# Projections with a contraction of 64: from a zero-padded 128-row matmul to two 64-row tiles

## The chip, the core and the metric

The kernel runs on one core of one Trainium2 chip. The time is device microseconds of that core, from several runs; beside it there is one profiled execution, from which all views of the trace come.

## What is computed

A linear attention with a feature map, and a gated feed-forward layer on its output. Shapes: q, k, v are 8 batches x 8 heads x 576 positions x 64; `w_phi` is 64 x 128; the feed-forward layer takes 4608 x 512 through 512 x 1536 (twice) and 1536 x 512.

```python
def phi(x):
    proj = np.einsum('bhsd,df->bhsf', x, w_phi)              # contraction over 64
    proj = proj - np.max(np.abs(proj), axis=-1, keepdims=True)
    return np.concatenate([np.exp(proj), np.exp(-proj)], axis=-1)
q_p, k_p = phi(q), phi(k)
kv = np.einsum('bhsf,bhsd->bhfd', k_p, v);  z = np.sum(k_p, axis=2)
num = np.einsum('bhsf,bhfd->bhsd', q_p, kv)
den = np.einsum('bhsf,bhf->bhs', q_p, z)[..., None] + 1e-06
x = (num / den)                                              # to (4608, 512)
out = (np.maximum(x @ w_gate, 0) * (x @ w_val)) @ w_out
```

## The kernel before

**Tiles.** Of the 576 positions of a head 512 make four chunks of 128; the last 64 of two batches make one "mixed" block. Input blocks hold two chunks (or two heads, in the mixed blocks) of 64 columns side by side, 128 x 128. `transposed` (L126) turns four or eight such blocks on TensorE (L131) and copies them to SBUF (L135). A turned block then holds the first chunk's 64 features on partitions 0 to 63 and the second's on 64 to 127; the first is called even here, the second odd.

**Projection by rows.** `project_rows` (L138) multiplies a turned block (stationary, 128 x 128) by `w2` (L505), which is two 128-column halves: `w_phi` on the upper 64 rows with zeros below, and zeros above with `w_phi` on the lower 64. A matmul of 256 columns (L142) so gives both chunks of a block side by side; two of them fill one PSUM bank, and one `tensor_reduce` (L147) takes the four largest absolute values. A K item (`k_start`, `k_rows`, `k_values`, `k_kv`) calls it twice, and each call is followed on ScalarE by two exponentials of 512 columns (L177, `kp`); after the second come two small ones of the maxima (L184, `ek`). A K item covers two heads of one batch; there are 32, and four mixed ones. `k_values` scales V by `ek` on GpSimd (L159), and `k_kv` (L204) sums 20 matmuls (L218).

**Projection by columns.** A Q item needs the rows only for its maxima (`q_rows`, L229; `cq`, L233), and the projection itself by columns: `q_cols` (L235) has one half of `w2` as the stationary operand and four turned blocks, 512 columns, as the moving one (L241), then two exponentials (L247, `qp`). A Q item covers two chunks of a batch and all heads: four row calls and four column calls. There are 16, and four mixed ones with half of that. `q_num` (L253) then does 16 matmuls of 65 columns a chunk (L263), VectorE adds the two halves (L279, L287) and takes a reciprocal (L290), GpSimd scales (L292, `xu`), and `q_finish` (L296) turns the result (L299, L305) into `xT`.

**Feed-forward.** `ffn_slices` (L309) cuts a batch's layer into slices: 12 pairs of a val and a gate slice, four matmuls of 512 columns each (L320), and twelve slices of four matmuls for the output (L342; a bank is taken by the first of three). A val slice is copied by ScalarE (L329), a gate slice is worked off by VectorE (L331). For batch 0 half of the pairs are cut into slices of 256 columns.

**What sets the order.** Nothing reorders: `at(tick, fn, ...)` puts each step on a fixed grid, and all steps are issued in the order of ticks (L576), at the same tick in the order of entry. From tick 36 on each tick has one feed-forward slice. A K item starts every four ticks: transposes at t0, row calls at t0+2 and t0+3, V at t0+5, `k_kv` at t0+10 (L389). A Q item has row calls at t0+2 to t0+5 and column calls at t0+4 to t0+7 (L420); the first two have ticks by hand (L518 to L527). PSUM has five banks under the tag `pa` for the attention (`ps_a`) and three under `pf` (`ps_f`), taken in turn.

Of the kernel before, what the change touches and what calls it, by code (L numbers as in the profile page):

```python
# [8 lines left out]
FP32 = mybir.dt.float32  # L9
BF16 = mybir.dt.bfloat16  # L10
# [6 lines left out]
def kernel(  # L17
# [24 lines left out]
    P = 128  # L42
# [92 lines left out]
        nc.vector.tensor_copy(t.rearrange("p a b -> p (a b)"), pt[:, 0 : n * P])  # L135
        return t

    def project_rows(T2, m):  # L138

        pp = psum_a()  # L140
        for i in range(2):
            nc.tensor.matmul(  # L142
                pp[:, 2 * F * i : 2 * F * (i + 1)],
                lhsT=T2[:, i, :],
                rhs=w2.rearrange("p a f -> p (a f)"),
            )
        nc.vector.tensor_reduce(  # L147
            m,
            pp.rearrange("p (c f) -> p c f", f=F),
            axis=AX.X,  # L150
            op=ALU.max,
            apply_absolute_value=True,
        )
        return pp

    def scale_v(engs, dst, src, ek):

        for s, eng in enumerate(engs):
            eng.tensor_tensor(  # L159
                dst[:, :, s, 0:D],  # L160
                src,
                ek[:, :, s : s + 1].to_broadcast([P, 8, D]),
                op=ALU.mult,
            )
        engs[0].tensor_copy(dst[:, :, :, D], ek)
# [4 lines left out]
        st["kp"] = []  # L170
        st["m"] = sb_s.tile([P, 8], FP32, name="mk")

    def k_rows(st, i):
        pp = project_rows(st["T"][:, 2 * i : 2 * i + 2], st["m"][:, 4 * i : 4 * i + 4])
        kp = st["pool"].tile([P, 2, 4, F], BF16, name=f"kp{i}")
        for s, sign in ((0, 1.0), (1, -1.0)):
            nc.scalar.activation(  # L177
                kp[:, s].rearrange("p c f -> p (c f)"), pp, AF.Exp, scale=sign
            )
        st["kp"].append(kp)  # L180
        if i == 1:
            ek = st["ek"] = sb_s.tile([P, 8, 2], FP32, name="ek")
            for s, sign in ((0, -1.0), (1, 1.0)):
                nc.scalar.activation(ek[:, :, s], st["m"], AF.Exp, scale=sign)  # L184

    def k_values(st, b, u, engs):
        vs = st["vs"] = sb_k.tile([P, 8, 2, E], BF16, name="vs")
        vn = inputs["vn", b][:, 2 * u : 2 * u + 2].rearrange("p h c d -> p (h c) d")
        scale_v(engs, vs, vn, st["ek"])

    def k_values_mixed(st, i, bb, engs):

        ekm = sb_s.tile([P, 8, 2], FP32, name="ekm")
        nc.vector.tensor_scalar(
            ekm.rearrange("p a b -> p (a b)"),
            st["ek"].rearrange("p a b -> p (a b)"),
            half[:, bb : bb + 1],
            None,
            op0=ALU.mult,
        )  # L200
        vs = st["vs", bb] = sb_mix.tile([P, 8, 2, E], BF16, name=f"vsm{bb}")
        scale_v(engs, vs, inputs["vm", i], ekm)

    def k_kv(st, b, u, copy):  # L204
        mixed = km_state[b // 2]
        pk = psum_a()
        kv_ps = pk[:, 0 : 4 * E].rearrange("p (h s e) -> p h s e", h=2, s=2)
        n = 0
        for hh in range(2):
            h = 2 * u + hh  # L210
            for s in range(2):
                for c in range(C + 1):
                    if c < C:
                        lhsT, rhs = st["kp"][hh][:, s, c, :], st["vs"][:, 4 * hh + c, s, :]
                    else:
                        lhsT = mixed["kp"][h // 4][:, s, h % 4, :]
                        rhs = mixed["vs", b % 2][:, h, s, :]
                    nc.tensor.matmul(  # L218
                        kv_ps[:, hh, s, :], lhsT=lhsT, rhs=rhs, start=(n == 0), stop=(n == 19)
                    )  # L220
                    n += 1
        kv = kvs[b, u] = sb_kv.tile([P, 2, 2, E], BF16, name="kv")
        copy(kv.rearrange("p h s e -> p (h s e)"), pk[:, 0 : 4 * E])  # L223

    def q_start(st, blocks):
        st["T"] = transposed(blocks)
        st["m"] = sb_s.tile([P, 2 * len(blocks)], FP32, name=f"mq{len(blocks)}")

    def q_rows(st, i):  # L229
        project_rows(st["T"][:, 2 * i : 2 * i + 2], st["m"][:, 4 * i : 4 * i + 4])  # L230
        if 4 * i + 4 == st["m"].shape[1]:
            st["c"] = sb_s.tile(st["m"].shape, FP32, name="cq")
            nc.scalar.activation(st["c"], st["m"], AF.Exp, scale=2.0)  # L233

    def q_cols(st, x, slot, lo, par, first):  # L235

        if "qp" not in x:
            x["qp"] = sb_f.tile([P, 2, 2, 4, P], BF16, name="qp", bufs=4)
            x["u"] = sb_f.tile([P, 8, E], FP32, name="u")
        pf = psum_f() if first else psum_a()  # L240
        nc.tensor.matmul(  # L241
            pf,
            lhsT=w2[:, par, :],
            rhs=st["T"][:, lo : lo + 4].rearrange("p a b -> p (a b)"),
        )
        for s, sign in ((0, 1.0), (1, -1.0)):
            nc.scalar.activation(  # L247
                x["qp"][:, s, slot].rearrange("p a b -> p (a b)"), pf, AF.Exp, scale=sign
            )

    GROUPS = ((0, 3), (3, 3), (6, 2))

# [136 lines left out]
    def k_item(t0, b, u, t_kv=0, engs=POOL, copy=nc.scalar.copy):  # L389
        st = {}  # L390

        def start():
            kn = inputs["kn", b]
            blocks = [
                kn[:, 2 * u + i // 2, 2 * (i % 2) : 2 * (i % 2) + 2, :].rearrange("p c d -> p (c d)")
                for i in range(4)
            ]
            k_start(st, blocks, sb_k)

        at(t0, start)  # L400
        at(t0 + 2, k_rows, st, 0)
        at(t0 + 3, k_rows, st, 1)
        at(t0 + 5, k_values, st, b, u, engs)
        at(max(t0 + 10, t_kv), k_kv, st, b, u, copy)

    def k_item_mixed(t0, i, engs=POOL):
        st = km_state[i] = {}

        def start():
            km = inputs["km", i]  # L410
            blocks = [km[:, 2 * j : 2 * j + 2, :].rearrange("p h d -> p (h d)") for j in range(4)]
            k_start(st, blocks, sb_mix)

        at(t0, start)
        at(t0 + 2, k_rows, st, 0)
        at(t0 + 3, k_rows, st, 1)
        at(t0 + 6, k_values_mixed, st, i, 0, engs)
        at(t0 + 22 if i else 44, k_values_mixed, st, i, 1, POOL)

    def q_item(t0, blocks, cols, chunks, ticks=None, **how):  # L420


        n = len(chunks)
        if ticks is None:
            ticks = dict(
                rows=[t0 + 2 + i for i in range(2 * n)],
                cols=[t0 + 4 + i for i in range(2 * n)],
                num=[t0 + 6 + 2 * n + 3 * ci for ci in range(n)],
                end=[t0 + 12 + 2 * n + 3 * ci for ci in range(n)],
            )  # L430
        st, xs = {}, [{} for _ in chunks]
        at(t0, lambda: q_start(st, blocks()))
        for i in range(2 * n):
            at(ticks["rows"][i], q_rows, st, i)
            ci, slot, lo, par = cols[i]
            at(ticks["cols"][i], q_cols, st, xs[ci], slot, lo, par, bool(how))
        for ci, (batches, place, col, dst) in enumerate(chunks):
            for j in range(3):
                at(
                    ticks["num"][ci] + j,  # L440
                    *(q_num, st, xs[ci], j, batches, place, col, how.get("t_act", False)),
                )
            at(ticks["end"][ci], lambda x=xs[ci], dst=dst: q_finish(x, dst()))
            last["q"] = ticks["end"][ci]

    def q_item_chunks(t0, b, cp, **how):
# [6 lines left out]
        def dst(c):  # L453
            if b not in xTs:
# [3 lines left out]
        q_item(  # L458
            t0,
            blocks,  # L460
            [(ci, half_, 4 * half_, ci) for ci in range(2) for half_ in range(2)],
            [
                (
                    (b,),
                    lambda h: (h // 4, h % 4),
                    lambda h, ci=ci: 2 * h + ci,
                    lambda ci=ci: dst(2 * cp + ci),
                )
                for ci in range(2)
# [4 lines left out]
    def q_item_mixed(t0, i):  # L474
        def blocks():
# [3 lines left out]
        q_item(  # L479
            t0,  # L480
            blocks,
            [(0, par, 0, par) for par in range(2)],
            [
                (
                    (2 * i, 2 * i + 1),
# [16 lines left out]
    load_v(0, 2, H, nc.gpsimd)  # L502
    load_mixed(0, "km", k, nc.gpsimd, BF16)
    load_q(0)
    w2 = singles.tile([P, 2, F], BF16)  # L505
    nc.vector.memset(w2, 0.0)
    half = singles.tile([P, 2], FP32)
    nc.vector.memset(half, 0.0)
    for hh in range(2):
        rows = slice(D * hh, D * (hh + 1))  # L510
        nc.vector.memset(half[rows, hh : hh + 1], 1.0)
        nc.vector.tensor_copy(w2[rows, hh, :], wf[rows])


    for u in range(NU):
# [1 line left out]
    k_item_mixed(16, 0, DVE)  # L517
    q_item_chunks(  # L518
        *(17, 0, 0),
        ticks=dict(cols=[20,20,20,21], rows=[20, 20, 22.5, 22.5], num=[27,30], end=[33.5,35]),  # L520
        t_act=True,
    )
    q_item_chunks(
        *(19, 0, 1),
        ticks=dict(cols=[33,33,34,34], rows=[26,29,32,35], num=[39,42], end=[45,47.5]),
        t_act=False,
    )  # L527
    S0 = 36
# [79 lines left out]
```

## Time and profile before

| | |
|---|---|
| median of 3 runs | 430.24 us (429.47 to 430.27) |
| span of the profiled execution, first to last instruction | 426.3 us |
| between that span and the median of the runs | 3.9 us |
| TensorE busy | 398.7 us, 94%, 3357 records of matmuls |
| VectorE busy | 284.1 us, 67% |
| ScalarE busy | 250.9 us, 59% |
| GpSimd busy | 159.6 us, 37% |
| granted TensorE clock, mean | 0.998 |

The profile page gives, in order, the busy time of each engine, the same in forty slices of the span (10.7 us each, tenths of busy), the DMA queues, and the chain of work that ended last. A line of a timeline has the start in us from the span's start, the length, the engine, the line of the kernel, the operation, the tiles (written <- read) and the number of instructions merged into it. Matmuls overlap in their records: the length of one is more than its distance to the next. A few records of matmuls are missing (a group of four may show three).

### The profile page before, as it was taken

How to read it: one execution, taken by the hardware profiler on the slowest of the kernel's cores; microseconds unless marked ns; L12 is line 12 of the kernel's file. 1: busy time of each engine (PE TensorE's matmuls, PEld its weight loads, DVE VectorE, ACT ScalarE, POOL GpSimd, SP SyncE). 2: the span in 40 equal slices, each digit the busy share in tenths (PEclk: the TensorE clock that was granted, in tenths of full speed). 3: DMA queues.
4: the chain of work that ended last, by engine and by line, in shares of the span. 5: the costliest groups of instructions: out<-in, count | busy, mean ns of one | idle time of the engine just before them, and what ended most of it. 6: DMA issues, size and time to landing. Idle time of an engine off the chain costs nothing.

```text
span 426.3 us, 8695 instructions
## 1 busy us (share of the span) xinstructions
PE 398.7 (94%) x3357; PEld 232.9 (55%) x3416; DVE 284.1 (67%) x641; ACT 250.9 (59%) x575; POOL 159.6 (37%) x204
## 2 busy tenths in 40 slices
PE   3777899989999999999999999999999999999995
PEld 1556665645556556555566556555565554444442
DVE  4888569867687679866876699676856795330420
ACT  3984776566667755687567665766667552322321
POOL 8953861176217501574155211870362021000000
PEclk9999999999999999999999999999999999999999
DMA  8997795245413750167015901374020002002004
GB/s 157 199 265 164 108 181 61 75 122 59 56 51 98 128 61 2 61 156 94 2 59 160 116 3 52 71 139 51 26 76 2 1 14 86 2 0 100 0 2 98
DMA packets 45337, 33.66 MB, mean 79 GB/s; under 512 B 12848, under 2 KB 40112, under 8 KB 45296
## 3 DMA queue, kind: packets, MB, share of 16 engines
q0 software_dynamic: 30480, 16.52, 28.1%
q1 hardware_dynamic: 14816, 16.58, 12.4%
q8 instruction: 27, 0.44, 0.4%
q14 instruction: 14, 0.11, 0.1%
HBM read 37.81 MB, written 9.44 MB: 111 GB/s over the span
## 4 chain that ended last, share of the span: by engine, by line
PE 78%; DVE 10%; ACT 4%; POOL 2%; issue 2%; DMA 2%; POOLq 0%; DVEq 0%; ACTq 0%
PE pf L320 40%; PE pf L342 17%; PE pa L142 6%; PE pa L218 5%; PE pa L263 4%; PE pa L241 3%; PE pa L131 3%; DVE u L287 2%; DVE mk L147 2%; DMA qn_117<-in_q_dram 2%; DVE t L279 2%; PE pa L299 1%; POOL xu L292 1%; ACT qp L247 1%; ACT t L275 1%
## 5 line engine op out<-in xcount | busy, mean ns | idle before, releaser
L320 PE MATMUL pf<-xT,wv_sb 128*128 128x512 bf16 (+1 forms) x386 | 96.9, 366 | 3.8 <-DVE xT L305 2.6
L320 PE MATMUL pf<-xT,wg_sb 128*128 128x512 bf16 (+1 forms) x394 | 97.7, 366 | 2.0 <-ACT val_sb L329 1.4
L292 POOL TENSOR_TENSOR xu<-u,r 128x512 bf16<-128x512 f32 x36 | 37.5, 1042 | 164.1 <-DVE r L290 128.9
L329 ACT CAST val_sb<-pf 128x512 bf16<-128x512 f32 (+1 forms) x114 | 65.3, 573 | 52.7 <-PE pf L320 52.3
L247 ACT ACTIVATE qp<-pa 128x512 bf16<-128x512 f32 x128 | 69.5, 604 | 11.9 <-PE pa L241 11.9
L320 PEld LDWEIGHTS <-wg_sb 128*128 128x128 bf16 x456 | 44.4, 98 | 41.6 <-issue 2.1
L320 PEld LDWEIGHTS <-wv_sb 128*128 128x128 bf16 x456 | 43.3, 98 | 36.5 <-issue 3.9
L147 DVE TENSOR_REDUCE mk<-pa 128x4 f32<-128x512 f32 x72 | 48.4, 682 | 11.3 <-PE pa L142 11.1
L263 PEld LDWEIGHTS <-qp 128*128 128x128 bf16 x640 | 33.9, 98 | 21.5 <-issue 0.9
L287 DVE TENSOR_TENSOR u<-pa,t 128x195 f32<-128x195 f32 (+3 forms) x120 | 40.5, 338 | 6.8 <-ACT t L275 0.5
L279 DVE TENSOR_TENSOR t<-pa,cq 128x195 f32<-128x195 f32 (+3 forms) x114 | 37.6, 330 | 4.6 <-PE pa L263 3.8
L352 ACT COPY out_sb<-pf 128x512 f32<-128x512 f32 x36 | 21.3, 592 | 32.4 <-PE pf L342 29.5
L263 PE MATMUL pa<-kv,qp 128*128 128x65 bf16 x640 | 37.9, 193 | 0.9 <-DVE u L287 0.5
L331 DVE SCALAR_TENSOR_TENSOR h_6277<-pf,val_sb 128x512 bf16<-128x512 f32 x12 | 8.3, 692 | 22.8 <-PE pf L320 22.8
L331 DVE SCALAR_TENSOR_TENSOR h_6056<-pf,val_sb 128x512 bf16<-128x512 f32 x12 | 8.3, 692 | 14.5 <-PE pf L320 14.5
L299 PEld LDWEIGHTS <-xu 128*128 128x128 bf16 x144 | 10.7, 98 | 11.7 <-POOL xu L292 3.8
L223 ACT CAST kv<-pa 128x260 bf16<-128x260 f32 x28 | 10.7, 380 | 10.0 <-PE pa L218 9.9
L299 PE MATMUL pa<-ident,xu 128*128 128x128 bf16 x144 | 14.0, 219 | 2.1 <-POOL xu L292 1.6
L331 DVE SCALAR_TENSOR_TENSOR h_566<-pf,val_sb 128x256 bf16<-128x256 f32 (+1 forms) x18 | 9.1, 506 | 8.8 <-ACT val_sb L329 4.1
L331 DVE SCALAR_TENSOR_TENSOR h_1578<-pf,val_sb 128x512 bf16<-128x512 f32 x12 | 8.3, 691 | 9.6 <-ACT val_sb L329 5.7
L305 DVE COPY xT<-pa 128x512 bf16<-128x512 bf16 x32 | 13.3, 417 | 1.9 <-PE pa L299 1.7
L331 DVE SCALAR_TENSOR_TENSOR h_3132<-pf,val_sb 128x512 bf16<-128x512 f32 x12 | 8.2, 686 | 7.3 <-PE pf L320 3.8
(580 smaller groups left out, 776.1 us busy)
## 6 DMA issues: line engine op xcount, KB each, us to landing
out_dram<-out_sb SPq DMA_DIRECT2D x32, 256.0 KB, 2.3
wv_sb<-in_moe_w_val_dram POOLq DMA_DIRECT2D x3, 512.0 KB, 8.2
wg_sb<-in_moe_w_gate_dram POOLq DMA_DIRECT2D x3, 512.0 KB, 9.7
wo_sb<-in_moe_w_out_dram POOLq DMA_DIRECT2D x1, 1536.0 KB, 13.3
vn_1018<-in_v_dram SPq DMA_DIRECT2D x1, 1024.0 KB, 8.9
vn_335<-in_v_dram POOLq DMA_DIRECT2D x1, 1024.0 KB, 13.5
vn_1793<-in_v_dram SPq DMA_DIRECT2D x1, 1024.0 KB, 7.1
vn_2508<-in_v_dram SPq DMA_DIRECT2D x1, 1024.0 KB, 7.2
```

The source lines that it names most:

```text
L142: nc.tensor.matmul(pp[:, 2 * F * i : 2 * F * (i + 1)], lhsT=T2[:, i, :], rhs=w2.rearrange("p a f -> p (a f)"),)
L147: nc.vector.tensor_reduce(m, pp.rearrange("p (c f) -> p c f", f=F), axis=AX.X, op=ALU.max, apply_absolute_value=True,)
L247: nc.scalar.activation(x["qp"][:, s, slot].rearrange("p a b -> p (a b)"), pf, AF.Exp, scale=sign)
L263: nc.tensor.matmul(pn[:, E * (2 * i + s) : E * (2 * i + s + 1)], lhsT=x["qp"][:, s, slot, blk, :], rhs=kvs[b, h // 2][:, h % 2, s, :],)
L279: nc.vector.tensor_tensor(t, ab[:, :, 1], st["c"][rows, col(lo) : col(lo + n - 1) + 1 : col(1) - col(0)][:, :, None].to_broadcast([np_, n, ...
L287: nc.vector.tensor_tensor(x["u"][rows, lo : lo + n], ab[:, :, 0], t, op=ALU.add)
L292: nc.gpsimd.tensor_tensor(x["xu"], x["u"][:, :, 0:D], r.to_broadcast([P, 8, D]), op=ALU.mult)
L299: nc.tensor.matmul(pt[:, P * i : P * i + P], lhsT=x["xu"][:, 2 * i : 2 * i + 2].rearrange("p a d -> p (a d)"), rhs=ident, is_transpose=True,)
L320: nc.tensor.matmul(ps, lhsT=w[:, dc, P * fi : P * fi + P], rhs=xT[:, dc, lo:hi], start=(dc == 0), stop=(dc == NDC - 1),)
L329: nc.scalar.copy(st["val"], ps)
L331: nc.vector.scalar_tensor_tensor(st["h2"][:, fi, lo:hi], ps, 0.0, st["val"], op0=ALU.max, op1=ALU.mult)
L342: nc.tensor.matmul(st["po"], lhsT=st["h2"][:, fi, P * t : P * t + P], rhs=wo_sb[:, fi, :], start=(fi == 0), stop=(fi == NFC - 1),)
```

## The change

The projections no longer multiply by zeros. `wd` holds `w_phi` twice, on partitions 0 to 63 and on 64 to 127. Each matmul takes 64 partitions of the turned block and of `wd`: the even chunk from the upper half, the odd one from the lower half. In the built program these have a tile of 64 rows x 128 columns at row 0 or row 64; all other matmuls keep 128 x 128. Even and odd chunks go to two PSUM banks.

Since a bank now holds four even or four odd chunks, `project_rows` takes four blocks at once and issues eight matmuls of 128 columns and two reduces; the two row calls of a K item become one, at t0+2, and all four exponentials and both `ek` come from that one step. Row and column calls of a Q item are paired in the same way (t0+2 and t0+4; t0+4 and t0+6). The order of V's blocks, of the maxima and of the stationary blocks of `k_kv` follows. The grid of all other steps stays.

```diff
-    def project_rows(T2, m):
-        pp = psum_a()
-        for i in range(2):
-            nc.tensor.matmul(
-                pp[:, 2 * F * i : 2 * F * (i + 1)],
-                lhsT=T2[:, i, :],
-                rhs=w2.rearrange("p a f -> p (a f)"),
-            )
-        nc.vector.tensor_reduce(m, ...)
-        return pp
+    def project_rows(T4, ms):
+        pps = [psum_a(), psum_a()]
+        for i in range(4):
+            for par in range(2):
+                half_rows = slice(D * par, D * (par + 1))
+                nc.tensor.matmul(
+                    pps[par][:, F * i : F * (i + 1)],
+                    lhsT=T4[half_rows, i, :],
+                    rhs=wd[half_rows, :],
+                )
+        for pp, m in zip(pps, ms):
+            nc.vector.tensor_reduce(m, ...)
+        return pps
...
-    def k_rows(st, i):
-        pp = project_rows(st["T"][:, 2 * i : 2 * i + 2], st["m"][:, 4 * i : 4 * i + 4])
-        kp = st["pool"].tile([P, 2, 4, F], BF16, name=f"kp{i}")
-        for s, sign in ((0, 1.0), (1, -1.0)):
-            nc.scalar.activation(kp[:, s]..., pp, AF.Exp, scale=sign)
-        st["kp"].append(kp)
-        if i == 1:
-            ek = ...
+    def k_rows(st):
+        pps = project_rows(st["T"], [st["m"][:, 4 * i : 4 * i + 4] for i in range(2)])
+        for i, pp in enumerate(pps):
+            kp = st["pool"].tile([P, 2, 4, F], BF16, name=f"kp{i}")
+            for s, sign in ((0, 1.0), (1, -1.0)):
+                nc.scalar.activation(kp[:, s]..., pp, AF.Exp, scale=sign)
+            st["kp"].append(kp)
+        ek = ...
...
-        vn = inputs["vn", b][:, 2 * u : 2 * u + 2].rearrange("p h c d -> p (h c) d")
+        vn = inputs["vn", b][:, 2 * u : 2 * u + 2].rearrange("p h (c a) d -> p a (h c) d", a=2)
...
-    def q_cols(st, x, slot, lo, par, first):
+    def q_cols(st, places, lo, first):
+        pfs = []
+        for x, slot in places:
...
+            pfs.append(psum_f() if first else psum_a())
+        for par, pf in enumerate(pfs):
+            half_rows = slice(D * par, D * (par + 1))
+            nc.tensor.matmul(
+                pf,
+                lhsT=wd[half_rows, :],
+                rhs=st["T"][half_rows, lo : lo + 4].rearrange("p a b -> p (a b)"),
+            )
+        for (x, slot), pf in zip(places, pfs):
+            for s, sign in ((0, 1.0), (1, -1.0)):
+                nc.scalar.activation(x["qp"][:, s, slot]..., pf, AF.Exp, scale=sign)
...
         at(t0, start)
-        at(t0 + 2, k_rows, st, 0)
-        at(t0 + 3, k_rows, st, 1)
+        at(t0 + 2, k_rows, st)
...
-                rows=[t0 + 2 + i for i in range(2 * n)],
-                cols=[t0 + 4 + i for i in range(2 * n)],
+                rows=[t0 + 2 + 2 * i for i in range(n)],
+                cols=[t0 + 4 + 2 * i for i in range(n)],
...
-    w2 = singles.tile([P, 2, F], BF16)
-    nc.vector.memset(w2, 0.0)
+    wd = singles.tile([P, F], BF16)
...
-        nc.vector.tensor_copy(w2[rows, hh, :], wf[rows])
+        nc.vector.tensor_copy(wd[rows, :], wf[rows])
...
-        ticks=dict(cols=[20,20,20,21], rows=[20, 20, 22.5, 22.5], num=[27,30], end=[33.5,35]),
+        ticks=dict(cols=[20, 20], rows=[20, 22.5], num=[27, 30], end=[33.5, 35]),
...
-        ticks=dict(cols=[33,33,34,34], rows=[26,29,32,35], num=[39,42], end=[45,47.5]),
+        ticks=dict(cols=[33, 34], rows=[26, 32], num=[39, 42], end=[45, 47.5]),
```

In the changed program the lines are some 3 to 16 higher: L144 is the row matmul, L150 its reduce, L182 and L188 the exponentials of a K item, L255 the column matmul, L262 its exponentials, L335 the val and gate matmuls, L344 the val copy.

## The prediction on record

> **What bounds the kernel now.** I read the page first: the share of each engine, then the slices, then the chain that ended last.
>
> ```profile
> span 426.3 us, 8695 instructions
> ...
> PE 398.7 (94%) x3357; PEld 232.9 (55%) x3416; DVE 284.1 (67%) x641; ACT 250.9 (59%) x575; POOL 159.6 (37%) x204
> ...
> PE   3777899989999999999999999999999999999995
> ...
> ACT  3984776566667755687567665766667552322321
> ...
> PE 78%; DVE 10%; ACT 4%; POOL 2%; issue 2%; DMA 2%; POOLq 0%; DVEq 0%; ACTq 0%
> ```
>
> From the fifth slice (some 42 us) TensorE is full, and the chain lies on it. "Busy" can mislead, so the timeline of TensorE alone comes next: there a matmul's real price is the distance to the next start.
>
> ```profile
> 202.73 0.35 PE L263 MATMUL pa<-kv,qp 128*128 128x65 bf16 x6
> 202.92 0.38 PE L142 MATMUL pa<-w_119,tT_3454 128*128 128x256 bf16 x2
> 203.14 1.03 PE L320 MATMUL pf<-xT,wv_sb 128*128 128x512 bf16 x4
> 204.00 0.35 PE L263 MATMUL pa<-kv,qp 128*128 128x65 bf16 x6
> ...
> 205.40 0.38 PE L241 MATMUL pa<-tT_3454,w_119 128*128 128x512 bf16 x1
> 205.61 0.38 PE L142 MATMUL pa<-w_119,tT_3454 128*128 128x256 bf16 x2
> 205.83 1.03 PE L320 MATMUL pf<-xT,wv_sb 128*128 128x512 bf16 x4
> ```
>
> Start to start: two L142 take 0.22 us, one L241 0.21, a slice of four L320 0.86, and six L263, each with a weight load of its own, 0.19 (0.031 for load and matmul). Nothing is idle between them, so a microsecond of TensorE work is worth a microsecond there, as long as nothing else becomes late. What could is ScalarE and the three PSUM banks `pf`, so I looked at one K item among val and gate slices:
>
> ```profile
> 188.08 0.38 PE L142 MATMUL pa<-w_119,tT_3208 128*128 128x256 bf16 x2
> ...
> 188.30 1.03 PE L320 MATMUL pf<-xT,wv_sb 128*128 128x512 bf16 x4
> 188.50 0.69 DVE L147 TENSOR_REDUCE mk<-pa 128x4 f32<-128x512 f32 x1
> ...
> 189.23 1.08 ACT L177 ACTIVATE kp_3255<-pa 128x512 bf16<-128x512 f32 x2 [0.57 <-DVE mk L147]
> ...
> 190.20 0.59 ACT L329 CAST val_sb<-pf 128x512 bf16<-128x512 f32 x1
> ...
> 190.66 1.12 ACT L177 ACTIVATE kp_3269<-pa 128x512 bf16<-128x512 f32 x2
> ...
> 191.56 0.81 PE L320 MATMUL pf<-xT,wg_sb 128*128 128x512 bf16 x3
> 191.63 0.34 ACT L184 ACTIVATE ek<-mk 128x8 f32<-128x8 f32 x2
> 191.83 0.62 ACT L329 CAST val_sb<-pf 128x512 bf16<-128x512 f32 x1
> ```
>
> The gate slice at 191.56 takes the bank of the val slice of 188.30 (three banks: val, gate, val, then the first again). The copy that frees it ends at 190.79, because it stands between the two pairs of exponentials. The margin is 0.77 us. ScalarE's pace, start to start: a pair 0.97, both `ek` 0.20, a copy 0.46 before the next may start, 0.59 to its end.
>
> **Edit 1: the streams get shorter.** 288 row matmuls of 256 columns become 576 of 128, in 72 calls; 72 column matmuls of 512 columns become 36 pairs. A rows call costs 4 x 0.108 = 0.43 now. Side by side its four pairs would stream in 4 x 0.056 = 0.22 (eight L131 transposes, also 128 columns wide, took 0.45 from 200.55 to 201.00), but it now has eight weight loads, and the L263 pace of 0.031 gives 0.25: 0.18 saved. A column pair costs 0.43 now and 0.215 + 0.03 (the second starts a load later) then: 0.185 saved. In the full region, after 42 us, there are 63 row calls and 32 column pairs; in 13 of the row calls the saving vanishes in a wait (edit 3). Gain: 50 x 0.18 + 32 x 0.185 = 14.9 us.
>
> **Edit 2: the array changes its shape.** The built order has the 64-row work in 90 separate stretches among 128-row work, 80 of them after some 42 us and 67 outside the 13 waits; each is entered and left, 134 changes. No row of this trace has a 64-row tile. Below, a change costs nothing, as between any two matmuls above (a gain is excluded: no work goes). Above, the earlier matmul must leave altogether and the next load cannot be early: a 65-column matmul lasts 193 ns and hands over after 31, so 0.16 us remain, and a load precedes its matmul by 0.03 (L241: load 205.37, matmul 205.40): 0.19. I take 0.12, nearer to the upper row, since a change is a wait for the one before and the zero rows are all of one shape: 134 x 0.12 = +16.1 us (0 to 25.5).
>
> The rule that speaks against the change stands in the Trainium skill, "TensorEngine Tiling (Array Packing)", section Key Properties: changing the tiling mode, not just the tile, drains TensorE. It gives no price; by the rule the upper row is the truer one (25.5), by the trace's unbroken streams it would be 0.
>
> **Edit 3: four exponentials in one piece.** `k_rows` now issues both reduces, four exponentials and both `ek` before the next slice is issued. ScalarE takes its work in order, so the val copy is queued behind all six; before, behind two. Worked out on the item above with 0.12 a change: row matmuls end at 188.08 + 0.12 + 0.25 = 188.45, and the first reduce starts 0.20 later (as 188.30 to 188.50); reduces to 189.33 and 190.01, first pair at 189.37, second at 190.34, `ek` at 191.31, copy from 191.51 to 192.1. TensorE leaves the 64-row work at 188.57 and wants that bank after 0.86 + 0.86 + 0.44 + 0.86, at 191.6; it gets it 0.5 late, 0.54 after the 191.56 of before. Behind the gate matmuls stand kv and all that follows. In the built order ten K items have the pattern rows, val, gate, transposes, val, gate; four of them have half as many transposes, so that their slice came 0.22 earlier: 6 x 0.54 + 4 x 0.76 = +6.3 us (5.1 with free changes, 7.0 with 0.19). K items among output slices are free of it, since `po` takes a bank once in three slices.
>
> Three K items of batch 1 stand among the half slices (256 columns). The chain of waits has exponentials at 47.28 (kp_836) and again at 51.16 (kp_914): 3.88 an item. Afterwards: 0.20 + 0.68 + 2 x 0.97 + 0.20 + val copy 0.37 = 3.4 until the bank is free, gate 0.43, kv 0.61, rows with two changes 0.49: 4.9. That is 3 x 1.0 = +3.1 us.
>
> **Edit 4: the start.** `cq` of the second Q item now stands ahead of the eight `qp` exponentials on ScalarE (all rows come at ticks 26 and 32, before the first columns at 33); it was last, at 32.36. It waits for two reduces that VectorE reaches after the reciprocal at 29.13: 29.33 + 2 x 0.65 = 30.65, `cq` to 31.0. The eight began at 28.54 and are on the chain until 32.68, where L320 waits for them: +2.3 us. Then at 38.05 the chain goes through `kp_660` to a val copy; that now waits for one more pair and `ek`: +1.2. Together +3.5 (0 to 5).
>
> **Free, and what hides it.** Counts and sizes of reduces, exponentials, V scalings and PSUM copies stay. V is read in another order with the same 64-element runs; POOL is busy 37%, and a call of 1.05 us could be longer by a tenth before `kv`, five ticks later, sees it. The dropped memset of `w2` lies under the first load. Column exponentials now come four in a row as well; TensorE's own work between the slices (num, kv) nearly covers them: +0.5 (0, where changes are dear, to 4, where they are free). No DMA moves on its queue.
>
> **Sum.** -14.9 + 16.1 + 6.3 + 3.1 + 3.5 + 0.5 = +14.6 on the profiled span of 426.3: 440.9. The median of the runs is 3.9 above that span (430.24), which I take as unchanged: **445 us**.
>
> **Rivals.** *The gain comes through (faster).* One mechanism: the val copies are not late, since ScalarE's 59% leaves room to catch up, and a change costs little. Without waits the streams give 63 x 0.18 + 32 x 0.185 = 17.3 against 160 changes; it decides at 0.108 a change. At 0.05 the sum is -9.3, 421 us. For it: the full TensorE row. Against it: the margin of 0.77, smaller than the pair and `ek` that are put before the copy. 11%. *No side by side*: the halves stream one after the other, or their loads do not overlap; edit 1 brings nothing, 460 us. For it: nothing in this trace shows two matmuls streaming at once. 12%. *Waits, but free changes*: -14.9 + 5.1 + 2.7 + 3.5 + 4 = +0.4, some 431 us, either side of no change. For it: the unbroken streams above, though all of one shape. 17% (5 faster, 6 within 0.2%, 6 slower). *Forecast*, with changes of 0.05 to 0.19: 436 (-14.9 + 6.7 + 5.6 + 2.9 + 3.5 + 2 = +5.8) to 454 (-14.9 + 25.5 + 7.0 + 3.3 + 3.5 = +24.4), 60%.
>
> **Numbers.** Likeliest 445. The range holds the forecast and most of the two cases beside it: 430 to 460. Faster by over 0.2%, about what a measurement here can tell from none: 16%; within 0.2%: 6%; slower: 78%.
>
> **What would show it.** Edit 1: a pair of L144 starting within some 0.03 us, rows calls of about 0.25, L255 pairs under 0.25. Edit 2: a gap before the first L144 or L255 of a stretch and before the first matmul after it. Edit 3: in K items TensorE idle before the second gate slice, released by the val copy. Edit 4: `cq` waiting for a reduce near 29 to 31 us and the first full slice 2 to 4 us later. Wrong would be: no gaps at the changes, or pairs one behind the other.

## The result, and the profile after

The changed kernel takes **448.93 us** (median of 4 runs, 447.95 to 449.15), the kernel before 429.86 us beside it (4 runs): ratio 1.0448, 95% interval 1.0429 to 1.0467. It is slower, as forecast, 3.9 us above the predicted 445.0 and inside the range.

From the page of the changed kernel: span, engine shares, two of the slices, granted clock and chain. They answer to the lines shown of before.

```profile
span 446.7 us, 9336 instructions
...
PE 405.0 (91%) x3704; PEld 225.5 (50%) x3704; DVE 282.8 (63%) x640; ACT 249.0 (56%) x575; POOL 159.7 (36%) x204
...
PE   2587679988999899999999999999999999999995
...
ACT  3954566546575765566666664676566662332321
PEclk9966899999999999999999999999999999999999
...
PE 67%; DVE 18%; ACT 10%; issue 2%; DMA 1%; POOL 0%; DVEq 0%; ACTq 0%; POOLq 0%
```

The profiled span grew by 20.4 us while VectorE's and ScalarE's busy times hardly moved. TensorE's share of the chain fell from 78% to 67%, and that of VectorE and ScalarE together rose from 14% to 28%: time went into waits for them. (TensorE's busy times can't be compared: the profile of before has 3357 matmul records for 3416 weight loads, so some are missing, this one has all 3704; and some matmuls run at half clock here.) The slices show two regions, a start that is emptier, at a lower clock in the third to fifth slice, and then a full TensorE again.

To see where the 20.4 us arise I followed the same slices through both traces, by VectorE's work on each gate slice: the changed kernel is 6.0 us behind at 33 us of before, 9.6 at 46, 12.0 at 58, and 20.4 from 342 on. **12.0 lie in the start, 8.4 in the steady part.**

The medians differ by 19.1 us and not by 20.4, because the profiled execution of before was a short one: its span is 426.3 us, those of the 43 executions of before listed with the experiments are 426.6 to 429.0. The traces show where. TensorE's waits for the first loads of K, before, in the changed kernel and in e13_qonly (the last experiment below):

```profile
PE pa L131 <- DMA kn_101<-in_k_dram: 5.6, 2, 4.5
PE pa L131 <- DMA kn<-in_k_dram: 7.2, 2, 4.8
PE pa L131 <- DMA kn<-in_k_dram: 6.5, 2, 4.7
```

(us in total, times, longest.) The second of these loads is issued at 2.67 us in all three; the transposes that it releases start at 7.74, 8.93 and 8.62 us. In all 13 profiled executions of other kernels they start at 8.2 to 9.0 us, also in e5_change and e13_qonly, which leave these first steps as they were. So 1.2 of the 12.0 us are, in all likelihood, not the change's.

TensorE's timeline of the changed kernel, over a K item (row call at 204.86) and a Q item:

```profile
204.86 0.40 PE L144 MATMUL pa<-wd,tT 64*128 64x128 bf16 x8
205.19 1.04 PE L335 MATMUL pf<-xT,wv_sb 128*128 128x512 bf16 x4
206.06 1.03 PE L335 MATMUL pf<-xT,wg_sb 128*128 128x512 bf16 x4
206.92 0.61 PE L131 MATMUL pa<-ident,qn 128*128 128x128 bf16 x8
207.37 1.03 PE L335 MATMUL pf<-xT,wv_sb 128*128 128x512 bf16 x4
208.79 1.02 PE L335 MATMUL pf<-xT,wg_sb 128*128 128x512 bf16 x4 [0.40 <-ACT val_sb L344]
...
210.23 0.20 PE L224 MATMUL pa<-vsm,kp 128*128 128x65 bf16 x1
210.35 0.40 PE L144 MATMUL pa<-wd,tT 64*128 64x128 bf16 x8
210.68 1.04 PE L335 MATMUL pf<-xT,wv_sb 128*128 128x512 bf16 x4
...
212.52 0.39 PE L255 MATMUL pa<-tT,wd 64*128 64x512 bf16 x2
212.74 0.39 PE L144 MATMUL pa<-wd,tT 64*128 64x128 bf16 x8
```

Three of the prediction's signs are here. *Side by side*: two L255 and then the next call within 0.22 us, the price of one full matmul of 512 columns; start to start, the two of a pair are 3 to 4 ns apart. The section "Part 3: Packing small matmuls — row/col tiling" of the Trainium skill's page "TensorE: Matmul & The Clock Gate" gives about 4 ns between the starts of packed tiles; this trace agrees. *Gaps at a change*: from the last L224 to the first L144 it is 0.12 us, where a 65-column matmul hands over after 0.031, so the way in costs 0.095; over all stretches I read 0.095 to 0.096 in, 0.092 to 0.102 out. *The late gate slice*: from 207.37 to 208.79 a slice takes 1.42 instead of 0.86 us, 0.56 late, released by the val copy.

The waits of TensorE in the changed kernel (us in total, times, longest), the whole span:

```profile
PE pf L335 <- ACT val_sb L344: 9.8, 13, 1.7
...
PE pf L335 <- DVE xT L320: 4.4, 4, 1.5
PE pf L255 <- ACT qp L262: 4.1, 2, 2.4
PE pa L144 <- DVE u L302: 3.7, 11, 0.4
```

The first line is what the prediction was built on. The last was not in it: the row call that directly follows a column pair waits for `u`, VectorE's add of a num step. TensorE's timeline, then VectorE's in the same stretch:

```profile
222.50 0.39 PE L255 MATMUL pa<-tT,wd 64*128 64x512 bf16 x2
222.73 0.22 PE L144 MATMUL pa<-wd,tT 64*128 64x128 bf16 x1
223.35 0.39 PE L144 MATMUL pa<-wd,tT 64*128 64x128 bf16 x7 [0.40 <-DVE u L302]
```

```profile
221.35 1.28 DVE L150 TENSOR_REDUCE mq<-pa 128x4 f32<-128x512 f32 x2
222.54 0.35 DVE L294 TENSOR_TENSOR t<-pa,cq 128x195 f32<-128x195 f32 x1
222.93 0.36 DVE L302 TENSOR_TENSOR u<-pa,t 128x195 f32<-128x195 f32 x1
```

The first even matmul goes; the first odd one waits for its bank. Of the five `pa` banks the stretch takes four, after one for a num step, so its last bank is that of the num step one tick back, and its reader `u` stands on VectorE behind two reduces in one piece (1.28 us). With the matmul that waits, all seven behind it wait. Ten such waits of 0.36 to 0.57 us after 60 us make 5.0 us.

### The profile page after: what moved, and what is told of

It reads as the page before. It is cut to its first block, busy times and chain, and to the rows that moved or that the text cites. A ratio compares the mean times of both kernels' runs of the same rounds, so it can differ in the third digit from the quotient of the medians.

```text
span 446.7 us, 9336 instructions
## 1 busy us (share of the span) xinstructions
PE 405.0 (91%) x3704; PEld 225.5 (50%) x3704; DVE 282.8 (63%) x640; ACT 249.0 (56%) x575; POOL 159.7 (36%) x204
## 4 chain that ended last, share of the span: by engine, by line
PE 67%; DVE 18%; ACT 10%; issue 2%; DMA 1%; POOL 0%; DVEq 0%; ACTq 0%; POOLq 0%
PE pf L335 33%; PE pf L357 18%; ACT kp L182 7%; PE pa L224 5%; PE pa L144 4%; DVE mk L150 4%; DVE u L302 3%; DVE mq L150 3%; DVE t L294 3%; PE pa L278 2%; PE pa L131 2%; DVE h L346 2%; PE pa L255 2%; ACT val_sb L344 1%; DMA kn<-in_k_dram 1%
## 5 line engine op out<-in xcount | busy, mean ns | idle before, releaser
L346 DVE SCALAR_TENSOR_TENSOR h<-pf,val_sb 128x512 bf16<-128x512 f32 (+1 forms) x114 | 75.4, 662 | 110.2 <-ACT val_sb L344 59.9
L335 PE MATMUL pf<-xT,wg_sb 128*128 128x512 bf16 (+1 forms) x408 | 100.9, 370 | 9.8 <-ACT val_sb L344 9.8
L335 PE MATMUL pf<-xT,wv_sb 128*128 128x512 bf16 (+1 forms) x408 | 101.9, 373 | 4.4 <-DVE xT L320 4.4
L357 PE MATMUL pf<-wo_sb,h 128*128 128x512 bf16 x432 | 105.0, 379 | 0.0
L182 ACT ACTIVATE kp<-pa 128x512 bf16<-128x512 f32 x144 | 74.4, 604 | 50.1 <-DVE mk L150 49.8
L344 ACT CAST val_sb<-pf 128x512 bf16<-128x512 f32 (+1 forms) x114 | 63.9, 577 | 56.0 <-PE pf L335 56.0
L162 POOL TENSOR_TENSOR vs<-vn,ek 128x512 bf16<-128x512 f32 x64 | 65.9, 1051 | 32.8 <-ACT ek L188 32.7
L262 ACT ACTIVATE qp<-pa 128x512 bf16<-128x512 f32 x128 | 66.1, 603 | 10.3 <-PE pa L255 10.3
L335 PEld LDWEIGHTS <-wg_sb 128*128 128x128 bf16 x456 | 43.4, 99 | 55.9 <-issue 13.1
L335 PEld LDWEIGHTS <-wv_sb 128*128 128x128 bf16 x456 | 39.4, 99 | 43.2 <-issue 8.1
L357 PEld LDWEIGHTS <-h 128*128 128x128 bf16 x432 | 37.8, 98 | 36.6 <-issue 0.5
L150 DVE TENSOR_REDUCE mk<-pa 128x4 f32<-128x512 f32 x72 | 46.2, 684 | 9.6 <-PE pa L144 9.5
L150 DVE TENSOR_REDUCE mq<-pa 128x4 f32<-128x512 f32 x72 | 45.8, 678 | 0.7 <-PE pa L144 0.2
L144 PE MATMUL pa<-wd,tT 64*128 64x128 bf16 x576 | 32.9, 228 | 8.4 <-DVE tT L135 4.4
L135 DVE COPY tT<-pa 128x512 bf16<-128x512 bf16 (+1 forms) x56 | 27.3, 487 | 5.9 <-PE pa L131 5.6
L144 PEld LDWEIGHTS <-tT 64*128 64x128 bf16 x576 | 19.1, 98 | 19.6 <-DVE tT L135 6.2
```

The lines of the kernel that those rows point to most:

```text
L144: nc.tensor.matmul(pps[par][:, F * i : F * (i + 1)], lhsT=T4[half_rows, i, :], rhs=wd[half_rows, :],)
L150: nc.vector.tensor_reduce(m, pp.rearrange("p (c f) -> p c f", f=F), axis=AX.X, op=ALU.max, apply_absolute_value=True,)
L162: eng.tensor_tensor(dst[:, :, s, 0:D].rearrange("p (a b) d -> p a b d", a=2), src, ek[:, :, s : s + 1].to_broadcast([P, 8, D]).rearrange(" ...
L182: nc.scalar.activation(kp[:, s].rearrange("p c f -> p (c f)"), pp, AF.Exp, scale=sign)
L262: nc.scalar.activation(x["qp"][:, s, slot].rearrange("p a b -> p (a b)"), pf, AF.Exp, scale=sign)
L335: nc.tensor.matmul(ps, lhsT=w[:, dc, P * fi : P * fi + P], rhs=xT[:, dc, lo:hi], start=(dc == 0), stop=(dc == NDC - 1),)
```

## The experiments

Theory: the loss is made of order (val copies behind four exponentials, `cq` ahead of the `qp` exponentials, second banks not yet free), and the change of shape takes back most of what the streams gain. Rivals: tiles are dear in themselves; the start is slow because of the clock. Every ratio is to runs of the kernel before beside them, whose medians were 429.1 to 429.5 us.

| run | edit | median us | ratio, 95% interval |
|---|---|---|---|
| e3_full | changed kernel, same steps, no tiles | 451.53 | 1.0498, 1.0467 to 1.0529 |
| e5_change | kernel before, columns from 64 rows, one at a time | 443.59 | 1.0326, 1.0297 to 1.0354 |
| e1_split | changed kernel, K exponentials in two steps | 437.06 | 1.0173, 1.0147 to 1.0199 |
| e2_cq | changed kernel, `cq` after the columns | 447.14 | 1.0408, 1.0380 to 1.0436 |
| e7_split_cq | both | 434.42 | 1.0113, 1.0081 to 1.0145 |
| e4_later | changed kernel, column pairs a tick later | 457.24 | 1.0651, 1.0635 to 1.0667 |
| e6_all | e7 and e4 | 443.13 | 1.0322, 1.0301 to 1.0344 |
| e8_warm | e6 and filler matmuls in the start | 444.02 | 1.0343, 1.0321 to 1.0365 |
| e11_early | e7, joined steps ahead of num | 433.47 | 1.0088, 1.0073 to 1.0102 |
| e10_hybrid | e11, no tiles in the start | 431.06 | 1.0035, 1.0023 to 1.0047 |
| e12_kfull | e10, no tiles in K items | 431.64 | 1.0049, 1.0036 to 1.0062 |
| e13_qonly | kernel before, tiles in steady Q items only | **427.80** | **0.9967, 0.9954 to 0.9979** |

**Order without tiles (e3_full).** Pairs, banks and steps as changed, matmuls zero-padded as before.

```diff
-                    lhsT=T4[half_rows, i, :], rhs=wd[half_rows, :],
+                    lhsT=T4[:, i, :], rhs=w2[:, par, :],
...
-                lhsT=wd[half_rows, :], rhs=st["T"][half_rows, lo : lo + 4]...
+                lhsT=w2[:, par, :], rhs=st["T"][:, lo : lo + 4]...
```

> The changed kernel with its steps, pairs, banks and orders, but each projection matmul uses all 128 rows and the zero-padded weights, as before the change: no 64-row tile, no change of shape. It separates the tiles from the rearrangement. Theory (the tiles by themselves gain a little, 20 us of streaming against 15 us of changes, and the rearrangement loses): TensorE streams 20 us more and has no gaps at changes, the waits stay; 448 to 454 us. Rival (the tiles are the loss): 430 to 438 us.

TensorE's waits in it:

```profile
PE pf L333 <- ACT val_sb L342: 10.4, 13, 1.7
...
PE pf L333 <- DVE xT L318: 4.9, 4, 1.8
...
PE pf L253 <- ACT qp L260: 4.6, 2, 2.3
```

The same waits, so they belong to the order. Tiles in this order are worth 2.6 us by the medians (451.53 against 448.93) and 1.1 by the two profiled spans, where followed slice by slice 3.2 us are gained after 58 us and 2.1 lost before. They are not the cause of the slowdown, as the theory had it (448 to 454 us).

**Changes of shape alone (e5_change).** Only the 64 rows without zeros, but each by itself: no pairs, no gain, two changes for each of the 72 column matmuls.

```diff
-            lhsT=w2[:, par, :],
-            rhs=st["T"][:, lo : lo + 4]...,
+            lhsT=w2[D * par : D * (par + 1), par, :],
+            rhs=st["T"][D * par : D * (par + 1), lo : lo + 4]...,
```

> The kernel before with one edit: a column matmul takes only the 64 rows that are not padded, still one at a time, so nothing is saved and each of the 72 is entered and left. Theory (a change of shape costs 0.096 us each way, as the gaps in the changed kernel show): 64 of them lie where TensorE is full, 64 x 0.19 = 12 us more, 441 to 443 us. Rival (a change is hidden, or costs only where something else waits): 430 to 433 us.

Its TensorE timeline:

```profile
203.63 0.39 PE L241 MATMUL pa<-tT,w 64*128 64x512 bf16 x1
203.95 0.39 PE L142 MATMUL pa<-w,tT 128*128 128x256 bf16 x2
204.18 1.03 PE L320 MATMUL pf<-xT,wv_sb 128*128 128x512 bf16 x4
205.13 0.39 PE L241 MATMUL pa<-tT,w 64*128 64x512 bf16 x1
```

From L241 to the next start 0.32 instead of 0.216, and from the slice of four at 204.18 to L241 0.95 instead of 0.86. 14.1 us over 72 stretches are 0.195 each, as the gaps add up (0.096 + 0.102). The time is 0.6 us above the range that I expected, which counted the 64 stretches of the full part alone. A lone row call or column pair, which saves 0.21, about breaks even; a column pair and a row call joined in one stretch save 0.43 and pay once.

**The K exponentials (e1_split) and `cq` (e2_cq), and both (e7_split_cq).**

```diff
-        pps = project_rows(st["T"], [st["m"][:, 4 * i : 4 * i + 4] for i in range(2)])
-        for i, pp in enumerate(pps):
+        st["pp"] = project_rows(st["T"], [st["m"][:, 4 * i : 4 * i + 4] for i in range(2)])
+        k_exp(st, 0)
+    def k_exp(st, i):
+        pp = st["pp"][i]
...
+        if i == 0:
+            return
         ek = ...
...
         at(t0 + 2, k_rows, st)
+        at(t0 + 3, k_exp, st, 1)
...
-        ticks=dict(cols=[33, 34], rows=[26, 32], num=[39, 42], end=[45, 47.5]),
+        ticks=dict(cols=[33, 34], rows=[26, 35], num=[39, 42], end=[45, 47.5]),
```

> The changed kernel, but the second pair of exponentials of a K item and its two small ones are issued one tick later, so that on ScalarE the val copy again stands between the two pairs. Theory (the waits for the val copy are the larger part of the loss): TensorE's waits for the val copy, 9.8 us in the changed kernel's trace, go, and the K items of the half slices get shorter; 436 to 441 us. Rival (the changes between 64 and 128 rows are the loss, and a wait removed here returns elsewhere): 446 to 449 us.

> The changed kernel, but the second row pair of the second Q item is at tick 35, after the columns, as its last row call was before. Theory (the start is late because cq holds up the eight exponentials): cq no longer stands ahead of them, the first gate slice is worked off some 2 us earlier than the 39 us of the changed kernel, and 445 to 447 us result. Rival (the start is held by something else, the granted clock for instance): 448 to 450 us.

> As the one with three orders mended, but the column pairs stay where the change put them (t0+4 and t0+6). Theory: 437.1 - 1.8 = 434 to 436 us, above the one with all three. Rival (the pair waits cost nothing beside the two others): the same time as with all three.

The waits of TensorE in e1_split:

```profile
PE pf L261 <- ACT qp L268: 3.9, 2, 2.2
PE pa L144 <- DVE u L308: 3.7, 11, 0.4
...
PE pf L341 <- ACT val_sb L350: 1.2, 3, 0.5
```

One step moved by a tick takes 11.9 us out: the val waits fall from 9.8 to 1.2 us, the start from 12.0 to 6.9, the steady part from 8.4 to 1.5. `cq` is worth 1.8 us alone (447.14, just above the theory's 445 to 447) and 2.6 on top of e1_split. What is left in e7_split_cq is 4.6 us at 58 us and 1.5 after, so most of it is start.

**Column pairs a tick later (e4_later, e6_all): a miss.** I wanted the row call's second bank to be free.

```diff
-                cols=[t0 + 4 + 2 * i for i in range(n)],
+                cols=[t0 + 5 + 2 * i for i in range(n)],
```

> The changed kernel, but the column pairs of a Q item come one tick later (t0+5 and t0+7), so that a row pair and a column pair no longer take four PSUM banks of the attention at once. Theory (the second bank of such a row pair waits for VectorE's add of the tick before, 5.1 us in all): those waits go, and the 14 stretches that were joined fall apart, 14 x 0.19 = 2.7 us more of changes; 445 to 448 us. Rival (VectorE is the bound there, so the wait only moves): 449 to 452 us.

> The changed kernel with three orders mended together: the second pair of exponentials of a K item one tick later, the second row pair of the second Q item at tick 35, the column pairs one tick later. Theory (the losses are separate waits and add up): 437.1 - 1.8 - 2.4, some 431 to 434 us; what is left above the kernel before lies in the first 50 us. Rival (they overlap): 435 to 438 us. If the tiles' own gain (20 us of streaming against some 18 us of changes) were larger than thought, under 429 us.

It costs 8.3 us alone and 8.7 on top of e7_split_cq, more than the rivals had allowed as well. TensorE in e6_all:

```profile
216.51 0.39 PE L261 MATMUL pa<-tT,wd 64*128 64x512 bf16 x1
217.27 0.39 PE L261 MATMUL pa<-tT,wd 64*128 64x512 bf16 x1 [0.37 <-DVE u L308]
217.59 1.04 PE L341 MATMUL pf<-xT,wg_sb 128*128 128x512 bf16 x4
```

Now the column pair meets the occupied bank. Its second matmul comes 0.76 us after the first and streams alone: the wait and, on top, the whole gain of the pair. 13 such waits sum to 6.6 us, where the row calls had lost 5.0 and have 1.1 now; 14 joined stretches fall apart into two (14 x 0.19 = 2.7). That is 6.6 - 3.9 + 2.7 = 5.4 of the 8.7, and 13 lost pairings of 0.21 make another 2.7.

**The clock in the start (e8_warm): not decided.** 17 times two throwaway matmuls of 512 columns before 30 us, in e6_all.

```diff
+    for wt in (0, 2, 4, 6, 8, 10, 12, 14, 16, 17, 18, 19, 24, 26, 27, 28, 29):
+        at(wt, warm, 2)
```

> The kernel with three orders mended, plus 17 times two throwaway matmuls of 512 columns on a spare bank in the first 30 us, which only keep TensorE busy. Theory (part of the late start is the granted clock, which falls to 0.5 for some 10 to 20 us since TensorE is idle there): the clock stays at 1.0 from some 18 us on and the span gets 2 to 4 us shorter than without them; 428 to 431 us. Rival (the start waits for other engines, the clock does not matter): the same time as without, or up to 3 us more for the throwaway work.

The rows of stretches (from:to, length, busy us of TensorE, weight loads, VectorE, ScalarE and GpSimd with their instructions, granted clock, share of DMA, GB/s) in the changed kernel say what it was for:

```profile
18.40:21.80 3.40, 1.01 (x16) 0.45 (x16) 3.37 (x5) 3.39 (x9) 3.38 (x6) 1.00 1.13 169
21.80:28.60 6.80, 6.21 (x102) 5.59 (x99) 4.48 (x11) 2.92 (x7) 2.58 (x5) 0.50 1.23 259
28.60:32.00 3.40, 2.26 (x42) 1.55 (x39) 2.71 (x8) 3.08 (x16) 0.67 (x1) 1.00 1.24 220
32.00:42.30 10.30, 7.52 (x46) 4.88 (x47) 5.06 (x14) 5.09 (x13) 2.92 (x4) 0.50 0.97 208
42.30:49.10 6.80, 4.19 (x58) 3.24 (x55) 5.04 (x17) 3.17 (x9) 1.78 (x2) 1.00 0.01 2
49.10:52.50 3.40, 3.11 (x24) 2.29 (x25) 2.19 (x5) 1.74 (x4) 3.40 (x5) 0.50 0.16 36
```

TensorE gets half its clock for 20.5 us, in three stretches. Those ahead of them show it less busy: 1.01 of 3.40 us, 2.26 of 3.40, 4.19 of 6.80. The kernel before keeps 1.00 from 18 to 45 us. The Trainium skill's page "TensorE: Matmul & The Clock Gate", section "Part 1: The HAM clock gate", states half rate after an idle window of about 3.4 us; the lengths here, 3.4, 6.8 and 10.3 us, fit its multiples, but TensorE was not idle in the stretches before. The filler did not hold the clock (0.87 from 18 to 45 us against 0.75 in e6_all, then 0.89 to 60 us against 1.00) and the time stayed, 444.02 against 443.13. What the clock adds to the start remains open: no run here changes the clock there by itself.

**The joined step ahead of num (e11_early), no tiles in the start (e10_hybrid), nor in K items (e12_kfull).**

```diff
-                rows=[t0 + 2 + 2 * i for i in range(n)],
-                cols=[t0 + 4 + 2 * i for i in range(n)],
+                rows=[t0 + 2 + 1.9 * i for i in range(n)],
+                cols=[t0 + 3.9 + 2.1 * i for i in range(n)],
...
+                    lhsT=T4[:, i, :] if padded or full["now"] else T4[half_rows, i, :],
+                    rhs=w2[:, par, :] if padded or full["now"] else wd[half_rows, :],
...
+    at(36, lambda: full.update(now=False))
```

> The version with the second K pair a tick later and cq after the columns, and in Q items the joined column and row step issued ahead of the num step of its tick (rows at t0+3.9, columns at t0+3.9 and t0+6). The second bank of that row pair is then one whose reader finished two ticks before, not the num bank whose add is still to come. Theory (the bank is what the row pair waits for): the waits of L144 for the add u, 5.0 us there, go, and the time falls from 434.4 to 429.5-432. Rival (VectorE is late anyway, the wait only moves to the num step or the next column pair): 433.5-435, with waits of the same sum at other lines.

> The version before this one in the list, and all projections issued before tick 36 as zero-padded 128-row matmuls, in the same paired steps and banks. In the start TensorE is not full, so 64-row streams save nothing there, but each change of shape lies in a chain of waits. Theory (changes cost in the start too): 1 to 2 us below the version it is made from, 428-431. Rival (the start's excess of 4.6 us is order alone, waits and clock): no difference, within 0.7.

> As the second of the list, but row matmuls of K items stay zero-padded 128-row ones all through; 64-row tiles only in Q items, where a column pair and a row pair stand together. Theory (0.096 on the way in and on the way out, 0.21 saved by a rows call): a stretch of one rows call is worth nothing, so this is within 0.7 of the second of the list. If changes are dearer beside K items than I read, faster by up to 3; if K tiles are a gain, slower by as much.

TensorE's waits after 60 us in e11_early:

```profile
PE pa L284 <- DVE u L308: 2.4, 9, 0.3
...
PE pa L144 <- DVE u L308: 0.6, 3, 0.2
```

Half of each theory: the row calls' waits go, but nine num steps now wait for the same add behind the two reduces, so 0.95 us are gained and not the 2.4 to 4.9 of the theory; the time is the rival's. Without tiles in the start another 2.4 us go, a little over what was expected: 10 stretches less, where TensorE is not full. K items with tiles or without differ by 0.6 us, as a lone stretch at break-even should.

**Tiles only where they are joined (e13_qonly).** The kernel before with both forms side by side; the third num step half a tick later, behind the slice, to give `u` time.

```diff
+        for i in range(0 if how else n):
+            at(ticks["rows"][i], q_rows_pair, st, i)
+            at(ticks["cols"][i], q_cols_pair, ...)
...
-                    ticks["num"][ci] + j,
+                    ticks["num"][ci] + j + (0.5 if j == 2 and ci == 0 and n == 2 and not how else 0),
```

> The kernel before, with 64-row tiles only in the Q items of the steady part (14 items of two chunks and four mixed ones): a column pair at t0+3.9 directly followed by a row pair, alone a row pair at t0+2 and a column pair at t0+6, and the third num step of the first chunk half a tick later, behind the slice. The start and all K items are those of before (two calls of 256-column matmuls, exponentials two by two). Theory (0.096 each way, 0.21 saved by a row call or a column pair, the rest of the loss in the start and in waits): 14 joined stretches at -0.24, some 33 lone ones at -0.02, waits for u at most +2: 425-428.5, not slower than before. Rival (VectorE stays late behind two reduces in one piece, or the paired exponentials delay the val copies of Q ticks): 429-431.5, with waits for u or val_sb in the steady part.

From its page, and its waits after 60 us:

```profile
span 425.7 us, 8954 instructions
...
PE 396.2 (93%) x3482; PEld 225.4 (53%) x3544; DVE 284.2 (67%) x643; ACT 249.7 (59%) x575; POOL 159.3 (37%) x204
```

```profile
PE pf L363 <- DVE xT L348: 1.5, 2, 1.2
PE pf L363 <- issue: 1.4, 9, 0.2
PE pa L142 <- DVE tT L135: 0.6, 3, 0.2
PE pf L363 <- ACT val_sb L372: 0.5, 1, 0.5
```

No wait for `u` is left in the list, and the val line is that of before in the same window (0.5, once). It is faster than before by 0.3%, and faster than the changed kernel by 21 us: 0.9 us behind by 33 us (TensorE's second load of K came 0.88 us later), 1.2 at 58, and 0.6 ahead at 377, 1.8 gained in the steady part. With the load left out that is 1.5 us ahead, as the medians say (427.80 against 429.28).

## Why the prediction was right, and where its sizes were off

The sign, the mechanism and the cause named first were right; the sum was +14.6 and is +19.1 by the medians. The 3.9 us added for the runs were no fixed distance: in the 43 executions of before the time is 1.7 to 2.2 us above the span of the same execution, and the rest of the 3.9 is that the profiled one was short. That the number came so near is in part luck: the terms below are off both ways, 5.8 us too dear and some 9 too cheap.

**Edit 1** was mis-sized: a row call takes 0.22 to 0.23 us, not 0.25. I priced eight weight loads at 0.031 each, but those of two tiles start 3 to 4 ns apart, as the matmuls do. A call saves 0.21, a pair 0.21: 50 x 0.214 + 32 x 0.214 = 17.5 us in place of 14.9 (2.6 better).

**Edit 2**: 0.096 a change, not 0.12. The 134 changes cost 12.9 in place of 16.1 (3.2 better). A change costs, as the rule on draining led one to expect, but half of the upper row. Whether TensorE is empty by then the trace doesn't show: the first 64-row matmul starts at 210.35, the record of the last one before it (0.20 from 210.23) ends at 210.43, and ends are modelled. That a stretch pays 0.19 for both ways, the upper row for one, is chance. What I left out are the changes of the start: counted at nothing, they cost 2.4 (e11_early to e10_hybrid).

Together, from 58 to 377 us of before, start to start on TensorE: streams -18.5, 148 changes +14.2, waits and small delays +12.6, sum +8.3 against 8.4 measured.

**Edit 3** held nearly to the digit. Six gate slices are 0.56 late (0.54 predicted); of the four predicted at 0.76, three are 0.78, and one is 1.54. The three items among half slices wait 1.05, 1.85 and 1.63 us where I had 1.0 each; why two of them wait longer I did not take apart. Predicted for both kinds and for the one more pair of edit 4 were 6.3 + 3.1 + 1.2 = 10.6, and e1_split takes out 11.9.

**Edit 4**, `cq`: 2.3 predicted, 1.8 (e2_cq) to 2.6 (e7_split_cq). Its sign is in ScalarE's timeline, later than I had it because the start was behind already:

```profile
34.08 0.22 ACT L243 ACTIVATE cq<-mq 128x16 f32<-128x16 f32 x1 [1.75 <-DVE mq L150]
34.20 4.00 ACT L262 ACTIVATE qp<-pf 128x512 bf16<-128x512 f32 x8
```

The start as a whole was **mis-sized** too: 12.0 us at 58 us, 10.8 without the late load of K, where edit 4 and the half slices had 6.6. With the load left out, the start is 6.2 us behind in e1_split, 4.2 in e7_split_cq, 4.1 in e11_early (the same start), 1.4 in e10_hybrid and 0.3 in e13_qonly, which has the start of before. So 4.6 us go with the K exponentials, 2.0 with `cq`, 2.7 with the changes of shape, and the 1.4 left in e10_hybrid are the pairing of steps and what the clock adds, which I did not separate.

**A missing term**: I checked the banks `pf` and not `pa`. The prediction said that counts and sizes of PSUM work stay, which is true, but each paired step takes two banks at once, and the second is not yet free: 5.0 us, the **largest miss**. This and the start (4.2 over) outweigh the 5.8 us by which edits 1 and 2 were better than I had them. The +0.5 for column exponentials has no counterpart: no slice after 60 us waits for `qp`.

**The rivals.** *No side by side* fell to starts 3 to 4 ns apart. *Waits, but free changes* fell to 0.096. *The gain comes through* named its condition rightly, no late val copies and a change below 0.108: the change is at 0.096, the copies were late. e13_qonly meets both conditions, in Q items alone, and is faster.

## What to carry to other kernels

Price a move to half-height tiles by stretch, not by matmul: here 0.19 us to go in and out, 0.21 saved by one pair of 512-column matmuls, so tiles pay only where several pairs stand together. Pairing takes two PSUM banks at once and hands its readers double work in one piece; before changing it, list for each tick which bank comes next, who reads it, and what stands ahead of that reader on its engine. Where a fixed grid is tight, a step that was in two halves should keep its two ticks even if the matmuls are joined.

## What the runs showed of the hardware that I had not expected

Eight weight loads of 64-row tiles with their eight matmuls of 128 columns cost little more than four full ones: 0.22 to 0.23 us for a row call, 0.22 for four L131 (228.29 to 228.52). If the second tile of a pair is held up (0.76 us in e6_all), the pair streams one after the other, so a late bank costs its wait and the saving. And a change directly from a column pair to a row pair, both of 64 rows, costs nothing: 0.222 to 0.224 us from start to start, though the moving operand and the stationary one change places.
